# The second network's selection: the mask is written by ScalarE into h's PSUM bank, and the predicated copy moves into the same step

## The chip, the cores and the metric

The kernel runs on one core of a Trainium2 chip. The metric is the device time of one execution in microseconds, from start to end; the median of the runs shown stands for the kernel. The profile is one execution of its own, whose span runs from the first to the last instruction of the program.

## The reference

Three stages follow each other. Attention pools pairs of queries and gives 2304 rows of 512. A router hands each row to one of 8 experts, 288 rows to each, and each expert applies its two matrices. The third stage, the second network, is applied to every row:

```python
def _moe2_ref(x, w_in, w_out):
    h = x @ w_in               # 2304 x 512 by 512 x 2048
    g = h - np.tanh(h)
    return g @ w_out           # 2048 x 512
```

All data are float32. The kernel keeps that precision by splitting each factor of a product into a high and a low part and adding three products.

## The kernel before

After attention the kernel takes the experts one by one. For each of the 8 it runs the expert's own two products (class FFN, `h1` and `y`) and then the second network on the expert's 288 rows. This second part is called a round here: round 0 is that of the first expert, round 7 that of the last. A round has 16 steps; step f handles 128 of the 2048 columns of h, as a tile of 128 partitions by 288 rows.

`stream` (L1067) sets TensorE's order. In step f it issues `stage_a` (12 products that leave h of step f in a PSUM bank; called A(f) here), then `stage_b` for the elementwise work, and from step 3 on `ostep(f - 3)` (12 products with the output weights, added up in four other banks; O(f - 3) here). TensorE's order is therefore A(0) A(1) A(2) A(3) O(0) A(4) O(1) and so on; O(13) to O(15) follow in the next expert's first products, and in the last round at the very end (`finale`). The banks of h come from a pool with two buffers (`hps`, L902): A(f + 2) can start only when everything that reads or writes the bank of step f is through.

The elementwise work finds g = h - tanh(h). The plain difference is exact enough only where h is large; elsewhere a polynomial in z = h² is used, and a predicated copy puts the difference over the polynomial where z is above T0². For one step the instructions are:

- ScalarE: z (L956), hc, a copy of h into SBUF (L957), th = tanh(h) (L958), s, the square of z plus a constant (L959), all read in that order; then gh, the high part of g (L975, the tile `ah`).
- GpSimd: th = hc - th (L960), and the low part of g (L976, the tile `al`; on VectorE in the very last step).
- VectorE: p in three products, called P1 (L961, reads hc and z), P2 (L965, reads z and p) and P3 (L967, reads s and p); the mask mk (L966); and the predicated copy SEL (L973).

`stage_b` calls `stage_c(f - 1)` after P1 of step f. So VectorE's order within a step is P1(f), SEL(f - 1), P2(f), mk(f), P3(f), ScalarE's is z(f), hc(f), th(f), s(f), gh(f - 1), and GpSimd's is th(f), low part of g(f - 1). Each engine takes its queue strictly in the order of the program.

Between the steps of a round the same engines carry other work: the router's search for the next expert's rows (VectorE, with some small products on TensorE and `sat` on ScalarE, in rounds 0 to 5), the next expert's gather (`gather`, L848, issued by GpSimd), its transposes (`xpose`, L859) and splits of weights (`split_w`, L838). Rounds 0 to 5 are called loaded here, rounds 6 and 7 quiet.

Of the kernel before, what the change touches and what calls it, by code (L numbers as in the profile page):

```python
# [10 lines left out]
F32 = mybir.dt.float32  # L11
F32R = mybir.dt.float32r
BF = mybir.dt.bfloat16
I32 = mybir.dt.int32
AF = mybir.ActivationFunctionType
OP = mybir.AluOpType
# [16 lines left out]
T0 = 0.45  # L33
LEAD = -0.018649105653569312
# [16 lines left out]
class Attention:  # L51
# [51 lines left out]
        self.t[P] = dict(kr=kr, qr=qr)  # L103

    def warm(self, n):
        """Products that nobody reads: the tensor engine's clock is slow until it has been busy for a while."""
        ps = self.t["warm"]
        for _ in range(n):
            self.nc.tensor.matmul(ps[:, 0, :128], self.idle, self.idle, start=True, stop=True)
# [295 lines left out]
class Router:  # L405
# [89 lines left out]
                                  skip_group_check=True)  # L495

    def warm(self, n):
        """Products that nobody reads: the tensor engine's clock slows down when it idles."""
        ps = self.spare()
        for _ in range(n):  # L500
            self.nc.tensor.matmul(ps[:, :128], self.ones, self.after, start=True, stop=True)
# [11 lines left out]
        v.tensor_tensor(A, key, km[:, :, None].to_broadcast([128, n, E]), op=OP.is_equal)  # L513

    def half(self, cs):
        """The start of the first search, for some of the tokens."""
        v = self.nc.vector
        n, K = len(range(TC)[cs]), 2 ** self.LEVELS0[0][1] - 1
        v.tensor_copy(self.Lm[:, cs], self.lg[:, cs])
        self.best(cs)  # L520
        v.tensor_tensor(self.G0[:, cs], self.m[:, cs, None].to_broadcast([128, n, K]),
                        self.top0.bitcast(F32)[:, None, :].to_broadcast([128, n, K]), op=OP.is_ge)
# [269 lines left out]
class FFN:  # L792
# [88 lines left out]
        self.x = xh, xl  # L881

    def mm3(self, steps, mode):
        """steps: (out, (w hi, w lo), (x hi, x lo), first of its sum, last of its sum); mode: what of it comes late."""
        n = len(steps)
        order = {"": [(j, p) for j in range(n) for p in range(3)],
                 "wx": [(j, p) for p in range(3) for j in range(n)],
                 "x": [(j, p) for j in range(n) for p in (0, 2)] + [(j, 1) for j in range(n)],
                 "w": [(j, p) for j in range(n) for p in (0, 1)] + [(j, 2) for j in range(n)]}[mode]
        seen = [0] * n  # L890
        for m, (j, p) in enumerate(order):
            if 2 * m == 3 * n:
                yield
            out, (wh, wl), (xh, xl), first, last = steps[j]
            self.nc.tensor.matmul(out, wl if p == 2 else wh, xl if p == 1 else xh, start=first and not seen[j],  # L895
                                  stop=last and seen[j] == 2)
            seen[j] += 1
# [54 lines left out]
    def stage_b(self, f, ps):  # L952
        nc = self.nc
        z, th, h, p = self.tmp("z", 2), self.tmp("th", 2), self.tmp("hc"), self.tmp("p", 2)
        s = self.tmp("s")
        nc.scalar.activation(z, ps, AF.Square)  # L956
        nc.scalar.activation(h, ps, AF.Copy)  # L957
        nc.scalar.activation(th, ps, AF.Tanh)  # L958
        nc.scalar.activation(s, z, AF.Square, bias=self.bias)  # L959
        nc.gpsimd.tensor_sub(th, h, th)  # L960
        nc.vector.scalar_tensor_tensor(p, h, LEAD, z, op0=OP.mult, op1=OP.mult)  # L961
        if f:
            self.stage_c(f - 1)
        mk = self.tmp("mk")
        nc.vector.scalar_tensor_tensor(p, z, ROOT, p, op0=OP.add, op1=OP.mult)  # L965
        nc.vector.tensor_scalar(mk.bitcast(I32), z, T0 * T0, None, op0=OP.is_gt)  # L966
        nc.vector.scalar_tensor_tensor(p, s, QUAD[1], p, op0=OP.add, op1=OP.mult)  # L967
        self.t[f] = p, mk, th

    def stage_c(self, f, quick=False):  # L970
        nc = self.nc
        p, mk, th = self.t.pop(f)
        nc.vector.copy_predicated(p, mk.bitcast(I32), th)  # L973
        gh, gw = self.g[f] = self.pair()
        nc.scalar.activation(gh, p, AF.Copy)  # L975
        (nc.vector if quick else nc.gpsimd).tensor_sub(gw, p, as32(gh))  # L976
# [30 lines left out]
            yield "e", 2  # L1007

    def finale(self, f):
        """The last step of the last expert's sums, and its rows' way out."""  # L1010
        nc = self.nc
        oT = self.wk.tile([128, DC, CAP], F32, name="oT", tag="yl")
        ps = [self.psum.tile([128, 512], F32, name=n, bufs=b) for n, b in (("ax2", 1), ("h", 2), ("h", 2))]
        g = self.g.pop(f)
        copies = (nc.scalar.copy, nc.vector.tensor_copy)
        cut = lambda d: slice(d * 128, d * 128 + 128)
        row = lambda j: slice(j * 96, j * 96 + 96)

        def turn(ds):
            for j in range(3):  # L1020
                for d in ds:
                    nc.tensor.transpose(ps[j][:96, cut(d)], oT[:, d, row(j)], self.ident)

        step = lambda d: (self.acc[d], (self.wo[0][:, f, cut(d)], self.wo[1][:, f, cut(d)]), g, False, True)
        for ds in ((0, 1), (2,), (3,)):
            for _ in self.mm3([step(d) for d in ds], "x"):
                pass
            for d in ds:
                if d < DC - 1:
                    copies[d % 2](oT[:, d], self.acc[d])  # L1030
                else:
                    for j in range(3):
                        nc.scalar.copy(oT[:, d, row(j)], self.acc[d][:, row(j)])
            if ds[0]:
                turn((ds[0] - 2,))
        turn((2, 3))
        for j in range(3):
            orow = self.wk.tile([96, DM], F32, name="orow", tag="row", bufs=3)
            copies[j % 2](orow, ps[j][:96])
            nc.gpsimd.memset(self.spacer, 0.0)  # L1040
            st = nc.gpsimd.indirect_dma_start(
                out=self.out, out_offset=bass.IndirectOffsetOnAxis(ap=self.pids[:, j:j + 1], axis=0),
                in_=orow, in_offset=None)
            for s in self.stores:
                self.tc.declare_no_dep(st.ins, s, reason="other rows")
            self.stores.append(st.ins)
# [159 lines left out]
def build(ctx, tc, q, k, v, w_gate, w1, w2, w_in, w_out, out):  # L1206
    nc = tc.nc
# [5 lines left out]
    ident = cst.tile([128, 128], F32, name="ident")  # L1213
    make_identity(nc, ident)
    lg = cst.tile([128, TC, E], F32, name="lg")
    bias = cst.tile([128, 1], F32, name="bias")
    spacer = cst.tile([1, 1], F32, name="spacer")
    with ExitStack() as c2:
        psum = c2.enter_context(tc.tile_pool(name="psA", bufs=1, space=bass.MemoryType.PSUM))
# [4 lines left out]
        def weights():  # L1224
            nc.gpsimd.memset(iw, 0.0)
            for s in range(2):
                r = slice(64 * s, 64 * s + 64)
                nc.gpsimd.tensor_copy(iw[r, :, s, :D], ident[r, None, r].to_broadcast([64, HP, D]))
                nc.sync.dma_start(iw[r, :, s, D:], w_gate.rearrange("(hp s d) e -> s d hp e", s=2, d=D)[s])
            nc.vector.memset(bias, QUAD[0])  # L1230
            router.fill()

        at.begin, at.later = weights, router.setup
# [48 lines left out]
```

## Time and profile before

| | us |
|---|---|
| median of 3 runs (1432.44 to 1438.55) | 1432.45 |
| span of the profiled execution | 1429.9 |
| TensorE products busy in it | 1266.8 (89%) |
| VectorE busy | 1189.8 (83%) |
| GpSimd busy | 787.2 (55%) |
| ScalarE busy | 663.1 (46%) |

The profiled execution's own time is its span; the median lies 2.55 us above it, which is what stands around the first and the last instruction. Busy products are not products at their peak rate: the records' ends are modelled, and the granted clock of TensorE (mean 0.946 over the span) sets their pace. The page's 40 slices show TensorE at 80% or more of most slices, and VectorE at 80 to 90% until the last 200 us, where it falls to 50 to 70%.

### The profile page before, as it was taken

What the parts mean: (1) busy time and instruction counts of PE and PEld (TensorE: products, weight loads), DVE (VectorE), ACT (ScalarE), POOL (GpSimd) and SP (SyncE); (2) the same over time, 40 slices, a digit from 0 to 9 for tenths busy, and PEclk for the clock granted to TensorE, in tenths of its full rate; (3) what the DMA queues carried; (4) which work ended last, traced back from release to release, by engine and by line L of the source; (5) the groups of instructions that cost most, each with busy time, mean ns of one, the idle gap of its engine ahead of it and who ended that gap; (6) DMA issues with size and microseconds to landing.
All of it is one profiled execution on the core that took longest, in us unless ns stands there. A gap on an engine that the chain in (4) does not pass through costs nothing.

```text
span 1429.9 us, 26773 instructions
## 1 busy us (share of the span) xinstructions
PE 1266.8 (89%) x9379; PEld 1097.6 (77%) x9379; DVE 1189.8 (83%) x2500; ACT 663.1 (46%) x1700; POOL 787.2 (55%) x688
## 2 busy tenths in 40 slices
PE   7888889898888988957989999989899899899997
PEld 6666666566666666647889989889799899898996
DVE  6898988888888889986797897997977978958665
ACT  3444445354444544512445444454454444545554
POOL 4666666756666766612355364553643553646544
PEclk8989999899999999978999999999999999999999
DMA  8887888887778877335832013102111220131200
GB/s 207 198 202 184 188 200 200 192 181 173 192 188 197 191 187 183 100 107 170 302 113 81 18 55 99 44 26 84 54 46 54 55 80 19 54 112 48 83 9 18
DMA packets 164967, 175.02 MB, mean 122 GB/s; under 512 B 66400, under 2 KB 117600, under 8 KB 164832
## 3 DMA queue, kind: packets, MB, share of 16 engines
q1 hardware_dynamic: 161760, 163.86, 45.1%
q0 software_dynamic: 3072, 9.44, 2.2%
q8 instruction: 74, 1.21, 0.4%
q14 instruction: 61, 0.50, 0.1%
HBM read 100.16 MB, written 26.21 MB: 88 GB/s over the span
## 4 chain that ended last, share of the span: by engine, by line
PE 42%; DVE 37%; issue 10%; ACT 6%; POOL 3%; DMA 2%; SPq 1%; DVEq 0%; POOLq 0%; ACTq 0%
PE acc L895 10%; PE h L895 8%; PE pv L235 6%; DVE p L961 5%; DVE pm L196 5%; PE aux L192 4%; DVE p L973 4%; PE sc L218 3%; PE sc L217 3%; ACT ah L975 3%; DVE p L967 2%; DVE db L778 2%; DVE q L186 2%; DVE G L483 2%; POOL al L976 1%
## 5 line engine op out<-in xcount | busy, mean ns | idle before, releaser
L227 POOL TENSOR_TENSOR acc<-acc,E 128x576 f32<-128x576 f32 x217 | 319.5, 1497 | 70.5 <-ACT E L219 69.3
L219 ACT ACTIVATE E<-sc 128x288 f32<-128x288 f32 x576 | 219.2, 413 | 253.3 <-PE sc L218 227.6
L196 DVE TENSOR_REDUCE pm<-aux 128x1 f32<-128x384 f32 x432 | 216.8, 546 | 34.3 <-PE aux L192 31.9
L895 PE MATMUL h<-yh,wi 128*128 128x288 f32 x1024 | 228.8, 304 | 0.0
L976 POOL TENSOR_TENSOR al<-p,ah 128x288 fp32r<-128x288 f32 x127 | 128.5, 1012 | 162.0 <-ACT ah L975 162.0
L218 PE MATMUL sc<-q,k 128*128 128x288 f32 x576 | 178.1, 316 | 43.7 <-DVE q L186 43.6
L217 PE MATMUL sc<-q,k 128*128 128x288 f32 x576 | 189.7, 336 | 1.8 <-ACT E L219 1.8
L960 POOL TENSOR_TENSOR th<-hc,th 128x288 f32<-128x288 f32 x128 | 120.5, 942 | 121.0 <-ACT th L958 118.6
L895 PE MATMUL acc<-ah,wo 128*128 128x288 f32 x1024 | 170.0, 307 | 10.2 <-ACT ah L975 10.1
L895 PEld LDWEIGHTS h<-yh,wi 128*128 128x128 f32 x1024 | 174.1, 193 | 0.5
L192 PE MATMUL aux<-kh,qz 128*128 128x384 f32 x432 | 155.8, 377 | 20.2 <-DVE pm L196 12.0
L235 PE MATMUL pv<-E,vr 128*64 128x288 f32 x1152 | 173.7, 424 | 0.0
L895 PEld LDWEIGHTS acc<-ah,wo 128*128 128x128 f32 x1024 | 146.9, 194 | 28.5 <-issue 13.9
L975 ACT ACTIVATE ah<-p 128x288 fp32r<-128x288 f32 x128 | 56.9, 445 | 210.7 <-DVE p L973 210.7
L218 PEld LDWEIGHTS sc<-q,k 128*128 128x128 f32 x576 | 117.5, 204 | 48.0 <-DVE q L186 48.0
L895 PE MATMUL h<-yl,wi 128*128 128x288 f32 x512 | 149.4, 300 | 0.0
L217 PEld LDWEIGHTS sc<-q,k 128*128 128x128 f32 x576 | 116.8, 203 | 22.9 <-issue 15.5
L192 PEld LDWEIGHTS aux<-kh,qz 128*128 128x128 f32 x432 | 80.6, 192 | 64.7 <-DVE pm L196 38.2
L961 DVE SCALAR_TENSOR_TENSOR p<-hc,z 128x288 f32<-128x288 f32 x128 | 93.7, 732 | 40.0 <-ACT hc L957 20.6
L845 POOL TENSOR_TENSOR w1l<-w1r,w1h 128x512 fp32r<-128x512 f32 x64 | 83.5, 1307 | 71.2 <-ACT w1h L844 67.5
L235 PEld LDWEIGHTS pv<-E,vr 128*64 128x64 f32 x1152 | 76.2, 139 | 53.2 <-issue 23.4
L895 PEld LDWEIGHTS h<-yl,wi 128*128 128x128 f32 x512 | 97.8, 194 | 0.0
(245 smaller groups left out, 2721.6 us busy)
## 6 DMA issues: line engine op xcount, KB each, us to landing
k<-kh SPq DMA_DIRECT2D x64, 288.0 KB, 5.1
w1r<-in_moe_w_dram SPq DMA_DIRECT2D x64, 256.0 KB, 2.9
w2r<-in_moe_w_dram SPq DMA_DIRECT2D x64, 256.0 KB, 2.8
q<-qh SPq DMA_DIRECT2D x64, 144.0 KB, 2.6
k<-kl SPq DMA_DIRECT2D x32, 288.0 KB, 5.5
vr<-in_v_dram SPq DMA_DIRECT2D x16, 576.0 KB, 6.5
qr<-in_q_dram SPq DMA_DIRECT2D x30, 288.0 KB, 8.2
kr<-in_k_dram SPq DMA_DIRECT2D x30, 288.0 KB, 9.1
```

The costliest lines, as they stand in the source:

```text
L192: nc.tensor.matmul(ps, qz[:, blk * 128:blk * 128 + 128], kh[:, pc * 384:pc * 384 + 384], start=True, stop=True)
L196: nc.vector.tensor_reduce(pm[:, blk, pc:pc + 1], ps, axis=AX.X, op=OP.max)
L217: nc.tensor.matmul(ps, t["k1"][s][:, ks], t["q1"][:, s, qs], start=True, stop=False)
L218: nc.tensor.matmul(ps, t["k2"][s][:, ks], t["q2"][:, s, qs], start=False, stop=True)
L219: nc.scalar.activation(e[:, hf], ps, AF.Exp, scale=1.0 / 16.0)
L227: eng.tensor_add(a, a, e)
L235: nc.tensor.matmul(t["pv"][64 * s:64 * s + 64, hf, :HALF], t["vr"][:, s, c, :], t["E", c, s][:, hf], start=(c == 0), stop=(c == KC - 1), s ...
L895: self.nc.tensor.matmul(out, wl if p == 2 else wh, xl if p == 1 else xh, start=first and not seen[j], stop=last and seen[j] == 2)
L960: nc.gpsimd.tensor_sub(th, h, th)
L961: nc.vector.scalar_tensor_tensor(p, h, LEAD, z, op0=OP.mult, op1=OP.mult)
L975: nc.scalar.activation(gh, p, AF.Copy)
L976: (nc.vector if quick else nc.gpsimd).tensor_sub(gw, p, as32(gh))
```

## The change

In `stage_b` the predicated copy of step f is issued in step f, as the last of VectorE's work on it, and `stage_c(f - 1)` (now only gh and the low part of g) moves ahead of s(f) on ScalarE and ahead of th(f) on GpSimd. P1 reads h from its PSUM bank in place of hc. The mask mk on VectorE is removed: ScalarE writes relu(z - T0²) over h in h's own bank, and the predicated copy reads its bits from there. The copy hc stays, since GpSimd's subtraction reads it. The biases of s and of the new mask are given as numbers; the tile `bias` gets a second column and one more memset at the start of the kernel. Comments are emptied.

```diff
@@ stage_b @@
         nc.scalar.activation(z, ps, AF.Square)
         nc.scalar.activation(h, ps, AF.Copy)
         nc.scalar.activation(th, ps, AF.Tanh)
-        nc.scalar.activation(s, z, AF.Square, bias=self.bias)
-        nc.gpsimd.tensor_sub(th, h, th)
-        nc.vector.scalar_tensor_tensor(p, h, LEAD, z, op0=OP.mult, op1=OP.mult)
         if f:
             self.stage_c(f - 1)
-        mk = self.tmp("mk")
+        nc.scalar.activation(s, z, AF.Square, bias=QUAD[0])
+        nc.gpsimd.tensor_sub(th, h, th)
+        nc.vector.scalar_tensor_tensor(p, ps, LEAD, z, op0=OP.mult, op1=OP.mult)
+        nc.scalar.activation(ps, z, AF.Relu, bias=-T0 * T0)
         nc.vector.scalar_tensor_tensor(p, z, ROOT, p, op0=OP.add, op1=OP.mult)
-        nc.vector.tensor_scalar(mk.bitcast(I32), z, T0 * T0, None, op0=OP.is_gt)
         nc.vector.scalar_tensor_tensor(p, s, QUAD[1], p, op0=OP.add, op1=OP.mult)
-        self.t[f] = p, mk, th
+        nc.vector.copy_predicated(p, ps.bitcast(I32), th)
+        self.t[f] = p
@@ stage_c @@
-        p, mk, th = self.t.pop(f)
-        nc.vector.copy_predicated(p, mk.bitcast(I32), th)
+        p = self.t.pop(f)
         gh, gw = self.g[f] = self.pair()
@@ build @@
-    bias = cst.tile([128, 1], F32, name="bias")
+    bias = cst.tile([128, 2], F32, name="bias")
...
-            nc.vector.memset(bias, QUAD[0])
+            nc.vector.memset(bias[:, 0:1], QUAD[0])
+            nc.vector.memset(bias[:, 1:2], -T0 * T0)
```

## Rows read from the trace of the kernel before

**Rows 1.** Windows: stretch, length; busy (count) of PE, PEld, DVE, ACT, POOL; PEclk, DMA.
```profile
1093.39:1152.46 59.07, 52.24 (x402) 50.40 (x400) 55.18 (x134) 29.64 (x83) 32.38 (x33) 0.94 0.12 34
1284.38:1332.14 47.76, 44.67 (x338) 44.13 (x337) 39.59 (x77) 29.04 (x81) 30.33 (x32) 1.00 0.14 43
1368.06:1412.63 44.57, 44.57 (x336) 44.25 (x334) 34.63 (x73) 26.40 (x74) 25.50 (x28) 1.00 0.01 2
```

**Rows 2.** Waits of PE, 1093 to 1152: total us, times, longest.
```profile
PE aux L545 <- ACT sat L540: 2.9, 1, 2.9
```

**Rows 3.** Waits of PE, 1284 to 1332.
```profile
PE ax L866 <- DVE xl L878: 3.1, 1, 3.1
```

**Rows 4.** Groups by line from 575 us on: busy us, mean ns, idle before.
```profile
L961 DVE SCALAR_TENSOR_TENSOR p<-hc,z 128x288 f32<-128x288 f32 x128 | 93.7, 732 | 40.0 <-ACT hc L957 20.6 <-POOL al L976 19.3
...
L966 DVE TENSOR_SCALAR mk<-z 128x288 int32<-128x288 f32 x128 | 39.3, 307 | 0.0
...
L917 DVE SCALAR_TENSOR_TENSOR al<-h,ah 128x288 fp32r<-128x288 f32 x64 | 29.1, 455 | 49.5 <-ACT ah L916 49.3
```

**Rows 5.** Timeline, start of round 7: start us, us, engine, instruction, idle before.
```profile
1368.66 0.42 ACT L958 ACTIVATE th<-h 128x288 f32<-128x288 f32 x1
...
1368.81 0.46 DVE L961 SCALAR_TENSOR_TENSOR p<-hc,z 128x288 f32<-128x288 f32 x1 [1.44 <-ACT hc L957]
...
1369.16 0.80 POOL L960 TENSOR_TENSOR th<-hc,th 128x288 f32<-128x288 f32 x1 [11.55 <-ACT th L958]
...
1369.30 0.98 DVE L965 SCALAR_TENSOR_TENSOR p<-z,p 128x288 f32<-128x288 f32 x1
...
1370.42 0.45 DVE L967 SCALAR_TENSOR_TENSOR p<-s,p 128x288 f32<-128x288 f32 x1
...
1372.78 1.32 PE L895 MATMUL acc<-ah,wo 128*128 128x288 f32 x8
```

**Rows 6.** Timeline, a step of round 7.
```profile
1373.81 0.80 POOL L960 TENSOR_TENSOR th<-hc,th 128x288 f32<-128x288 f32 x1
1373.88 1.05 DVE L961 SCALAR_TENSOR_TENSOR p<-hc,z 128x288 f32<-128x288 f32 x1 [0.70 <-POOL al L976]
...
1374.85 0.48 DVE L973 COPY_PREDICATED p<-mk,th 128x288 f32<-128x288 int32 x1
...
1375.36 0.45 ACT L975 ACTIVATE ah<-p 128x288 fp32r<-128x288 f32 x1 [1.31 <-DVE p L973]
...
1375.81 0.45 DVE L967 SCALAR_TENSOR_TENSOR p<-s,p 128x288 f32<-128x288 f32 x1
...
1375.88 1.04 POOL L976 TENSOR_TENSOR al<-p,ah 128x288 fp32r<-128x288 f32 x1 [1.28 <-ACT ah L975]
```

**Rows 7.** Timeline of DVE, round 4: P3 of steps 1 and 2.
```profile
1098.34 0.45 DVE L967 SCALAR_TENSOR_TENSOR p<-s,p 128x288 f32<-128x288 f32 x1
...
1101.48 0.45 DVE L967 SCALAR_TENSOR_TENSOR p<-s,p 128x288 f32<-128x288 f32 x1
```

**Rows 8.** Timeline of DVE, round 4: step 7, and P1 of step 8.
```profile
1117.66 0.44 DVE L961 SCALAR_TENSOR_TENSOR p<-hc,z 128x288 f32<-128x288 f32 x1
1118.03 0.47 DVE L973 COPY_PREDICATED p<-mk,th 128x288 f32<-128x288 int32 x1
...
1118.98 0.44 DVE L967 SCALAR_TENSOR_TENSOR p<-s,p 128x288 f32<-128x288 f32 x1
...
1126.07 0.45 DVE L961 SCALAR_TENSOR_TENSOR p<-hc,z 128x288 f32<-128x288 f32 x1
```

**Rows 9.** Timeline of PE, round 4: tally products, and O(8).
```profile
1128.44 0.43 PE L494 MATMUL aux<-G,A 128*8 128x63 bf16 x9
...
1135.45 2.08 PE L895 MATMUL acc<-ah,wo 128*128 128x288 f32 x8
```

**Rows 10.** Windows (columns as in group 1), just after that wait.
```profile
1135.72:1139.12 3.40, 3.40 (x17) 3.39 (x17) 3.30 (x12) 1.43 (x5) 1.35 (x2) 0.50 0.01 5
```

**Rows 11.** Timeline of PE, the last O.
```profile
1417.80 0.79 PE L895 MATMUL acc<-ah,wo 128*128 128x288 f32 x4
```

## The prediction

> **What bounds the kernel now.** The change touches only the eight rounds of the second network, so I read the windows of the rounds first (from a round's first z to its last). In round 7 TensorE is never idle: 336 products in 44.57 us, 0.133 each, so 12 of them take 1.59 and a step (A and O) 3.18 [rows 1]. Round 6 is nearly the same. A loaded round, of which there are six, takes 59.07: VectorE is busy for 55.18 of them and TensorE for 52.24, at a mean clock of 0.94 [rows 1]. So two limits have to be kept apart: in quiet rounds TensorE, with the elementwise chain just keeping up; in loaded rounds VectorE's queue, for which TensorE waits in a few places, the longest 2.9 us for `sat` [rows 2]. Next I read the groups by line, for what each operation costs and whether something stretches it, and then the timelines of a round's start, of a quiet step and of loaded steps, for the order and the gaps.
>
> **Two facts about VectorE decide the sum.** First, an instruction with two SBUF inputs and a GpSimd subtraction exclude each other. P1 (two SBUF inputs) starts at 1373.88 while th runs until 1374.61, and ends at 1374.93, 0.32 after it, after 1.05 us [rows 6]; the mean of P1 is 732 ns where the undisturbed one takes 440 to 450 [rows 4, 8]. It holds the other way round as well: the low part of g starts at 1375.88 during P3 and ends at 1376.92, 0.66 after P3 [rows 6]. An instruction with one input in PSUM is free of this: 64 of L917 have a mean of 455 [rows 4]. Second, an instruction that doesn't need its predecessor's result starts before that one ends (SEL at 1118.03, P1 before it until 1118.10), while one that does starts after the end (P2 of step 0 at 1369.30, its P1 until 1369.27) [rows 5, 8]: 0.07 ahead against 0.03 behind.
>
> **What is removed and moved on VectorE.** mk goes: 307 ns [rows 4], but by starts only about 0.22 of VectorE's time. In exchange the order becomes P1, P2, P3, SEL, each needing the one before, where SEL of the previous step and mk stood between them until now. Block before, P1's start to P3's end: 1117.66 to 1119.42, 1.76 [rows 8]. Block after: 0.46 + 0.45 + 0.45 + 0.48 and three gaps of 0.03 to 0.04, 1.94 [rows 5, 6, 8]. So the block gets 0.18 longer, although it has one instruction fewer. What is won is that P1 no longer stands still behind GpSimd.
>
> **What is added on ScalarE.** The mask is one pass over 288 elements from SBUF. No row shows a write to PSUM by ScalarE; the nearest is gh, 0.45 [rows 6], and I take that; below it, 0.3, above it, 0.55. At either end ScalarE, busy for 29.6 of 59 us [rows 1], has room. But the mask waits for P1, and behind it in ScalarE's queue stand z of the next step, `sat` and the weights' splits. Before, gh(f - 1) held the same queue until SEL(f - 1), which came after P1(f); so this wait ends no later. s without its bias tile costs the same or less. The extra memset is one instruction outside the rounds, below 0.2 us. No DMA and nothing on SP moves.
>
> **The wait that is new.** SEL(f) now needs th(f) from GpSimd in the same step, and th(f) stands there behind the low part of g(f - 1), and behind any gather or split. Behind SEL wait all router instructions on VectorE. And A(f + 2) needs h's bank, which now is free after SEL(f) instead of after tanh(f). I follow this at three places.
>
> *Start of a round* (round 7, time from its first z at 1368.06 [rows 1]): tanh ends at 1.02, th runs on GpSimd from 1.10 to 1.90, P1 today starts at 0.75 [rows 5]. After: P1 takes h's bank after ScalarE's last read, 1.06 to 1.52; P2 is held by th and ends at 1.90 + 0.32 = 2.22; P3 to 2.71; SEL 2.75 to 3.23. A(2) starts at 3.27. (If the program lets P1 read h beside tanh, P1 starts at 0.44, behind z, SEL(0) ends at about 2.9, and the lateness found below is 2.9 in place of 3.2; I take 3.2, the order of one engine after the other on one bank.) Step 1: gh(0) to 3.71; P1 3.2 to 3.65; P2 to 4.15; low part of g held by P2, to 4.81; P3 to 5.13; th to 5.79; SEL to 6.33. A(3) runs from 6.37 to 7.96, then O(0). Today O(0) starts at 4.72 [rows 5], with A(1) to A(3) without a gap. TensorE is 3.2 us late, in two gaps of about 1.6.
> The Trainium skill, "PSUM — Partial Sum Buffer", section "PSUM bank collisions raise a hardware error", says that ScalarE and VectorE must not read one bank at the same time, which speaks against P1 on h beside tanh. No row shows such a pair; by this rule the later of the two starts above is the right one, and the sum stays.
>
> *A quiet step:* from the end of SEL(f - 1): gh to 0.48, P1 beside it to 0.39, P2 0.42 to 0.87, low part of g to 1.53, P3 to 1.85, th to 2.51, SEL to 3.05 to 3.2 by the order in which P3 and th get through. TensorE needs 3.18. So the chain just keeps up, and TensorE's lateness from the start stays to the end.
>
> *A loaded round.* Where the router has about 1 us of work in a step, today's step is 3.14 [rows 7]. After, P2 and P3 come to lie where the low part of g and th run: SEL ends 3.35 to 3.43 after the last SEL; I take 3.4, 0.26 more. Where the router has 2 us or more, GpSimd is done in time and the step is longer by the block alone, 0.18. Up to step 8 of round 4 there are four of each: 1.04 + 0.7. At step 0 VectorE is through at 3.23 instead of 2.81 (end of P3(0), 1370.87 [rows 5]), 0.4 more. Today P3(8) ends one block of 1.76 after 1126.07, that is 34.4 us into the round [rows 1, 8]; after, SEL(8) at 36.6. A(10) has to wait for it; then come O(7) and A(11), three times 1.59, and 1.3 of tallies and transposes (two tallies of 0.43 [rows 9] and as much again for the rest, an estimate): O(8) at 42.7. Today O(8) starts at 1135.45, 42.1 into the round [rows 9], because TensorE had stood for `sat` before. That wait goes, and the one for SEL(8) takes its place: 0.6 us late per loaded round.
>
> **The clock.** After the 2.9 us wait the granted clock was 0.50 for 3.4 us (the lower of the two levels, 1.2 GHz) [rows 10], which costs 1.7. After the 3.1 us wait of round 6 none fell: 1.00 throughout [rows 1, 3]. The two new gaps at a round's start add up to 3.2, the size of both; one of two is half, so I take 0.85 for each of 8 rounds (0 to 1.7).
>
> **The sum.** Six loaded rounds: 6 x 0.6 = 3.6. Round 7: TensorE late by 3.2, but its last O waits for gh today and starts at 1417.80 [rows 11]; A(15) ends 24 times 1.59 behind O(0) at 1372.78 [rows 5], at 1411.0; after, 3.2 later, and O(12) to O(14) follow without waiting, three times 1.59: 1419.0, 1.2 late. Round 6: 3.2, of which its 3.1 us wait [rows 3] can take up to all; half, 1.5. Clock: 8 x 0.85 = 6.8. Together 13.1. The profiled execution's span of 1429.9 becomes 1443.0, the median, 2.55 above it, about 1445. Low end: no clock loss, light steps at 3.1, round 6 at nothing: 1431. High end: light steps at 3.5, the lower clock in every round, 3.2 in round 6, and 1 us per loaded round where the next expert's first product waits for SEL(14): 1463.
>
> **Rivals.** *VectorE's relief wins (1417).* Per round mk is 16 x 0.307 = 4.9 and the excess of P1 is 16 x (0.732 - 0.455) = 4.4 [rows 4]. If the gaps between dependent instructions did not matter, a loaded round had 9.3 us less on VectorE; less the 3.2 of the start, half of the rest reaching TensorE, 3 per round: 18 gained, 2.7 lost in rounds 6 and 7. For it: VectorE is the fullest engine there. Against it: the starts in rows 5 and 8. The Trainium skill, "VectorE: DVE Perf Modes", "Rules for kernel authors", states for chained operations that a drain happens regardless and that the number of operations is to be made small; by this rule the shorter list is the faster one, and the rows on starts speak against it. Chance 0.22.
> *The waits only change places (1435).* The lateness of the start is taken up by the waits that TensorE has anyway, and the clock falls as often as now: 1432.45 + 1.2 + 1.5. For it: 6.8 us of idle TensorE in the loaded round. Chance 0.28, with anything from 1425 to 1439.
> *My forecast, slower (1445):* the mechanism is h's bank, held until SEL; it decides as soon as SEL(f) ends over 4.8 us (three times 1.59) after A(f), or A(2) would otherwise have followed at once. Chance 0.50.
> That the change doesn't do what it says, the mask costing ScalarE 0.55 in place of 0.45, alters none of these.
>
> **How the numbers follow.** 0.5% is about what a measurement of this kernel can tell from no change: 7.2 us, 1425.3 to 1439.6. Faster 0.22, same 0.28, slower 0.50. The range leaves out the best part of the first rival and the tip of the last: 1420 to 1460; the likeliest case's own range is 1431 to 1463.
>
> **What would show it.** In the trace after: A(2) and A(3) waiting for SEL (L973's successor) at the start of all eight rounds, O(0) near 8 us; P1 never over 0.5 us; P2 and P3 stretched to about 1 us in light steps; the wait for `sat` gone and one of some 4 us for SEL at step 8; round 7 at 47 to 48 us between first and last z plus its lag. Wrong would be: P2 starting before P1 ends, loaded rounds under 56 us, or A(2) following at once.

## The result, and the profile after

The changed kernel takes **1439.95 us** (median of 12 runs, 1434.93 to 1445.46) against 1432.45 of the kernel before, measured beside it: a ratio of **1.0053, 95% interval 1.0034 to 1.0071**. It is slower, by about as much as a measurement of this kernel can tell from no change. Its profiled execution spans 1438.9 us, 9.0 more than the one before. The attention part moves by up to 10 us from profile to profile (the first z of round 0 lies between 694.5 and 705.2 us in the kernels below), so I count from that z to the end: 729.7 us before, 739.3 after, **9.6 more**. From round to round the differences are +2.6, +1.0, +1.6, +0.1, +0.1, +0.6 for the loaded rounds 0 to 5, -0.1 for round 6 and +3.7 for round 7.

The windows of rounds 4, 6 and 7 from first to last z, with the columns of [rows 1] (length; busy us and count of PE, PEld, DVE, ACT, POOL; granted clock; DMA):

```profile
1098.10:1158.33 60.23, 52.94 (x421) 50.29 (x420) 52.26 (x119) 35.04 (x97) 30.18 (x33) 0.94 0.12 33
1289.81:1337.64 47.83, 44.82 (x338) 44.10 (x337) 39.25 (x63) 33.19 (x96) 30.64 (x33) 1.00 0.14 42
1373.35:1421.92 48.57, 46.17 (x326) 45.59 (x325) 37.32 (x59) 30.62 (x89) 26.22 (x29) 0.93 0.01 1
```

In the loaded round VectorE has 2.9 us less to do than in [rows 1], yet the round is 1.2 longer: VectorE now stands idle for 8.0 of its 60.2 us, against 3.9 of 59.1. The relief is there, and something eats it. The waits of PE in rounds 4 and 6 (total us, times, longest):

```profile
PE h L895 <- DVE p L967: 7.3, 5, 3.5
...
PE h L895 <- DVE p L967: 3.0, 2, 1.9
```

The wait for `sat` [rows 2] and round 6's wait of 3.1 [rows 3] are gone. In both rounds all that is listed is the first product of an A that waits for SEL, now line 967, to free h's bank. The groups by line from 575 us on, for [rows 4] (busy us, mean ns, idle before):

```profile
L962 POOL TENSOR_TENSOR th<-hc,th 128x288 f32<-128x288 f32 x128 | 123.0, 961 | 95.0 <-ACT th L958 95.0
L975 POOL TENSOR_TENSOR al<-p,ah 128x288 fp32r<-128x288 f32 x127 | 111.9, 881 | 204.9 <-ACT ah L974 196.8 <-PE acc L895 7.6
L966 DVE SCALAR_TENSOR_TENSOR p<-s,p 128x288 f32<-128x288 f32 x128 | 103.5, 809 | 13.4
L965 DVE SCALAR_TENSOR_TENSOR p<-z,p 128x288 f32<-128x288 f32 x128 | 94.3, 737 | 4.4
L967 DVE COPY_PREDICATED p<-h,th 128x288 f32<-128x288 int32 x128 | 62.4, 488 | 24.8 <-POOL th L962 9.7
L963 DVE SCALAR_TENSOR_TENSOR p<-h,z 128x288 f32<-128x288 f32 x128 | 57.6, 450 | 24.5 <-ACT th L958 24.0
...
L961 ACT ACTIVATE s<-z 128x288 f32<-128x288 f32 x128 | 56.2, 439 | 0.0
L964 ACT ACTIVATE h<-z 128x288 f32<-128x288 f32 x128 | 52.9, 414 | 69.1 <-DVE p L963 68.2
```

SEL, P2 and P3 of before, which [rows 4] does not show:

```profile
L973 DVE COPY_PREDICATED p<-mk,th 128x288 f32<-128x288 int32 x128 | 82.3, 643 | 0.8
...
L965 DVE SCALAR_TENSOR_TENSOR p<-z,p 128x288 f32<-128x288 f32 x128 | 63.4, 495 | 0.3
...
L967 DVE SCALAR_TENSOR_TENSOR p<-s,p 128x288 f32<-128x288 f32 x128 | 58.9, 460 | 0.0
```

P1 (L963) has a mean of 450 ns in place of 732 and a longest of 0.46 us: GpSimd never holds it any more. SEL, whose mask now lies in PSUM, falls from 643 to 488. P2 and P3 (L965, L966) are held instead, 737 and 809 ns in place of 495 and 460, since th and the low part of g now run beside them. So of the 95.3 us that mk, P1 and SEL are spared in the eight rounds, P2 and P3 take 75.5 back. The mask costs 414 ns on ScalarE, and s without its bias tile 439.

The idle time in round 4 has its own rows (P3, P2, SEL, P1):

```profile
L966 DVE SCALAR_TENSOR_TENSOR p<-s,p 128x288 f32<-128x288 f32 x15 | 12.2, 816 | 1.6
L965 DVE SCALAR_TENSOR_TENSOR p<-z,p 128x288 f32<-128x288 f32 x15 | 10.2, 679 | 0.5
L967 DVE COPY_PREDICATED p<-h,th 128x288 f32<-128x288 int32 x14 | 6.8, 486 | 1.8
L963 DVE SCALAR_TENSOR_TENSOR p<-h,z 128x288 f32<-128x288 f32 x15 | 6.7, 448 | 2.4 <-ACT th L958 2.4
```

Ahead of P2, P3 and SEL, each behind the one whose result it needs, VectorE stands idle for 3.9 us in all, where it had none before; that is nearly the whole of the 4.1 us by which its idle time in the round grew.

The start of round 7 (start us, us, engine, instruction, idle before):

```profile
1373.95 0.42 ACT L958 ACTIVATE th<-h 128x288 f32<-128x288 f32 x1
...
1374.40 0.46 DVE L963 SCALAR_TENSOR_TENSOR p<-h,z 128x288 f32<-128x288 f32 x1 [1.74 <-ACT th L958]
1374.45 0.80 POOL L962 TENSOR_TENSOR th<-hc,th 128x288 f32<-128x288 f32 x1 [11.55 <-ACT th L958]
...
1374.90 0.66 DVE L965 SCALAR_TENSOR_TENSOR p<-z,p 128x288 f32<-128x288 f32 x1
...
1375.66 0.46 DVE L966 SCALAR_TENSOR_TENSOR p<-s,p 128x288 f32<-128x288 f32 x1
...
1376.25 0.48 DVE L967 COPY_PREDICATED p<-h,th 128x288 f32<-128x288 int32 x1
...
1376.79 0.40 PE L895 MATMUL h<-yh,wi 128*128 128x288 f32 x1 [1.88 <-DVE p L967]
...
1379.78 0.61 PE L895 MATMUL h<-yh,wi 128*128 128x288 f32 x1 [0.52 <-DVE p L967]
```

P1 takes the bank 0.03 after tanh, P2 follows it by 0.04, P3 stands 0.10 behind P2 and SEL 0.13 behind P3; the next A has to wait for SEL twice. The windows of two of the seven stretches at the lower clock, from the first z on:

```profile
1132.00:1138.80 6.80, 5.48 (x35) 5.21 (x36) 5.13 (x10) 4.69 (x14) 4.01 (x5) 0.50 0.05 14
1377.80:1384.60 6.80, 6.28 (x27) 5.93 (x26) 4.50 (x7) 3.56 (x12) 3.31 (x5) 0.50 0.00 1
```

There are seven of 6.8 us. In rounds 0 to 4 one begins some 34 us in, during the wait of 3.5 us for SEL of step 8; in round 5 one begins at 30.4 us, during a wait of 4.1 for the router (`tot`); the last stands at the start of round 7. Before there were ten of 3.4 us like [rows 10]. Half of the 47.6 us against half of the 34.0 is 6.8 us more, and that is the most that the clock can have cost: TensorE was busy in 39.5 us of these stretches and waited in the rest, where before it was busy in nearly all of them. By the busy time alone the clock cost 2.8 us more.

### The profile page after: what moved, and what is told of

Its sections match the earlier page's. It is cut to its first block, busy times and chain, and to the rows that moved or that the text cites. A ratio compares the mean times of both kernels' runs of the same rounds, so it can differ in the third digit from the quotient of the medians.

```text
span 1438.9 us, 26644 instructions
## 1 busy us (share of the span) xinstructions
PE 1267.3 (88%) x9379; PEld 1096.2 (76%) x9379; DVE 1170.4 (81%) x2373; ACT 704.5 (49%) x1828; POOL 765.1 (53%) x688
## 4 chain that ended last, share of the span: by engine, by line
PE 42%; DVE 21%; issue 21%; POOL 9%; DMA 3%; ACT 3%; SPq 2%; POOLq 0%; DVEq 0%; ACTq 0%
PE h L895 10%; PE acc L895 9%; PE pv L235 6%; PE aux L192 5%; DVE pm L196 4%; POOL th L962 4%; PE sc L217 4%; PE sc L218 4%; POOL al L975 3%; DVE db L778 2%; DMA qr<-in_q_dram 1%; PE aux L164 1%; PE aux L298 1%; DVE q L186 1%; DVE G L483 1%
## 5 line engine op out<-in xcount | busy, mean ns | idle before, releaser
L895 PE MATMUL h<-yh,wi 128*128 128x288 f32 x1024 | 238.3, 312 | 47.1 <-DVE p L967 47.1
L975 POOL TENSOR_TENSOR al<-p,ah 128x288 fp32r<-128x288 f32 x127 | 111.9, 881 | 204.9 <-ACT ah L974 196.8
L895 PEld LDWEIGHTS h<-yh,wi 128*128 128x128 f32 x1024 | 177.2, 196 | 55.8 <-DVE p L967 54.7
L966 DVE SCALAR_TENSOR_TENSOR p<-s,p 128x288 f32<-128x288 f32 x128 | 103.5, 809 | 13.4
L186 DVE TENSOR_TENSOR q<-ident,nm 64x320 fp32r<-64x320 f32 (+1 forms) x64 | 98.0, 1532 | 1.6
```

The source lines that it names most:

```text
L186: nc.vector.tensor_mul(dv[oth[s], bs, hf, :], self.ident[r, None, r].to_broadcast([64, n, 64]), nm[r, bs, None].to_broadcast([64, n, 64]))
```

## The experiments

The theories were, in short: *the bank* (h's bank is held until SEL, TensorE starts every round late: my prediction), *dependent starts* (P1, P2, P3, SEL one behind the other cost VectorE what mk's removal saves), and against them *VectorE's relief* (P1 without GpSimd's hold is what counts). To compare them I read one quantity throughout: round 4 from its first to its last z, split into VectorE's busy and idle time.

| kernel | ratio to before | interval | round 4, us | VectorE busy | idle |
|---|---|---|---|---|---|
| before | 1 | | 59.07 | 55.18 | 3.89 |
| P1 from PSUM alone | 0.9877 | 0.9854–0.9900 | 54.54 | 51.25 | 3.29 |
| ScalarE's mask alone, in SBUF | 1.0015 | 0.9994–1.0036 | 59.46 | 52.61 | 6.85 |
| both | 0.9921 | 0.9895–0.9947 | 56.45 | 50.13 | 6.32 |
| both, SEL(f-1) ahead of P1(f) | 0.9921 | 0.9891–0.9952 | 56.61 | 52.85 | 3.76 |
| both, SEL(f) in its own step, th first | 1.0039 | 1.0018–1.0059 | 58.63 | 52.93 | 5.70 |
| both, SEL(f) in its own step | 1.0030 | 1.0013–1.0047 | 57.64 | 51.62 | 6.02 |
| the change (mask in h's bank) | 1.0053 | 1.0034–1.0071 | 60.23 | 52.26 | 7.97 |

**The bank freed after P1.** In the changed kernel the mask goes into a tile in SBUF.

```diff
-        nc.scalar.activation(ps, z, AF.Relu, bias=-T0 * T0)
+        mk = self.tmp("mk")
+        nc.scalar.activation(mk, z, AF.Relu, bias=-T0 * T0)
-        nc.vector.copy_predicated(p, ps.bitcast(I32), th)
+        nc.vector.copy_predicated(p, mk.bitcast(I32), th)
```

> The changed kernel with one edit: ScalarE writes the mask into an SBUF tile, so h's bank is free after P1(f) and not after SEL(f); order and number of instructions stay. My theory (the bank held until SEL is the cause): A(2) of a round starts at about 1.6 us in place of 3.4, O(0) at 5.5 to 6.5 in place of 8.4, the wait of A(10) at step 8 ends at P1's end, 1.7 us earlier; the half-clock stretch at the start of round 7 is gone; 1433 to 1436 us against the 1440 of the change. Rival (the longer chain SEL, gh, low part of g, th, SEL through GpSimd is the cause, whoever holds the bank): as the change, 1438 to 1442, since SEL now has two SBUF inputs and shares VectorE's lock with GpSimd.

Measured 1437.9 us, 1.0030. In round 7 A(2) follows at once (1.56 us after the first z, 3.44 in the changed kernel), and O(0) of a loaded round starts at 5.97 us in place of 8.39. Of the 3.4 us by which TensorE starts late (O(0) at 5.01 before), 2.4 are gone in rounds 1 to 5, and only about 0.2% comes back, with intervals that overlap. From round to round this profile is 0.8 to 1.5 us shorter than the changed kernel's in rounds 0 to 4; against that, round 6 is 4.1 longer, with a wait of 3.6 us for `xl` and a stretch of 6.8 at half speed that the changed kernel doesn't have there. So the late start exists as predicted, but with it gone the kernel is still slower than before: it is not the main cause of the loss.

**th ahead of the low part of g on GpSimd**, in the changed kernel:

```diff
+        nc.gpsimd.tensor_sub(th, h, th)
         if f:
             self.stage_c(f - 1)
         nc.scalar.activation(s, z, AF.Square, bias=QUAD[0])
-        nc.gpsimd.tensor_sub(th, h, th)
```

> The changed kernel with one edit: GpSimd subtracts th(f) before the low part of g(f - 1), so SEL(f) no longer waits for gh and the low part of the step before. My theory: A(2) unchanged (3.4), A(3) about 0.9 earlier, SEL(f) 0.5 to 0.9 earlier in every light step, no gain at step 8; 1435 to 1438. Rival (GpSimd's order is the whole cause): round starts near the old ones and 1433 or less. Rival (the order is without weight, the bank alone counts): 1440.

Measured 1438.34 us, 1.0030 (1.0015 to 1.0046). TensorE's waits for SEL sum up to 47.8 us, as in the changed kernel (47.1). So it is not th's place behind the low part of g that makes SEL late.

**P1 from PSUM, alone**, in the kernel before:

```diff
-        nc.vector.scalar_tensor_tensor(p, h, LEAD, z, op0=OP.mult, op1=OP.mult)
+        nc.vector.scalar_tensor_tensor(p, ps, LEAD, z, op0=OP.mult, op1=OP.mult)
```

> The kernel before with one part of the change alone: P1 reads h from PSUM; mask, SEL and order as before. My theory: P1 is never stretched by GpSimd any more (0.45 in place of a mean of 0.73), VectorE has 4 us less per round, but h's bank is held until P1 (about 1.5 to 2.3 us after z in place of 1.0, 6.7 at step 8); together little: 1429 to 1433. Rival (VectorE's relief decides): 4.4 us less on VectorE in each of six loaded rounds, half of it reaching the end: 1419 or less.

Measured **1417.34 us, 0.9877**: one operand, and 1.2% faster than the kernel before. I had given it next to nothing. Its window of round 4:

```profile
1087.28:1141.82 54.54, 50.73 (x402) 48.53 (x400) 51.25 (x134) 29.32 (x82) 31.82 (x33) 0.97 0.13 37
```

Its group of P1 from 575 us on:

```profile
L961 DVE SCALAR_TENSOR_TENSOR p<-h,z 128x288 f32<-128x288 f32 x128 | 57.7, 451 | 52.4 <-ACT th L958 45.2 <-POOL al L976 6.3 <-ACT s L959 0.9
```

VectorE has 3.9 us less to do in the round, its idle time stays, and the round is 4.5 shorter: in a loaded round what VectorE is spared reaches the end, if its idle time doesn't grow. P2 and P3 are not held in exchange (498 and 488 ns in this round). The clock goes from 0.94 to 0.97 with it: four stretches at half speed instead of ten are left. At 1.7 us each these six are some 10 of the 19.4 us by which this profile is shorter from the first z on, so up to half of the gain may come by way of TensorE's clock.

**ScalarE's mask, alone**, in SBUF, in the kernel before (mk on VectorE is dropped, `nc.scalar.activation(mk, z, AF.Relu, bias=...)` takes its place):

```diff
+        nc.scalar.activation(mk, z, AF.Relu, bias=-T0 * T0)
         nc.vector.scalar_tensor_tensor(p, z, ROOT, p, op0=OP.add, op1=OP.mult)
-        nc.vector.tensor_scalar(mk.bitcast(I32), z, T0 * T0, None, op0=OP.is_gt)
```

> The kernel before with another part alone: ScalarE makes the mask (relu of z less the threshold) into the SBUF tile mk, VectorE's mask instruction is gone; SEL stays in the next step. My theory: P3 now follows P2, whose result it needs, directly, and starts 0.1 after its end, where with mk between them it started 0.22 after mk's start; so VectorE's block shrinks by about 0.1 us a step only: 1430 to 1433. Rival (the number of VectorE instructions decides, as in the skill's rule on chained operations): 0.3 us a step, 4.9 a loaded round, half of it at the end: 1418 or less.

Measured 1434.74 us, 1.0015 with 1 inside the interval: no gain, and just above the range that I had given. Its round 4:

```profile
1094.44:1153.90 59.46, 52.92 (x421) 50.91 (x419) 52.61 (x119) 34.35 (x97) 32.21 (x33) 0.94 0.12 33
```

Its group of P3 in this round:

```profile
L967 DVE SCALAR_TENSOR_TENSOR p<-s,p 128x288 f32<-128x288 f32 x15 | 7.3, 487 | 1.6
```

VectorE does 2.6 us less and idles 3.0 more. More than half of the new idle time stands ahead of P3, which now follows directly on P2, whose result it needs (1.6 us in 15 steps, 0.0 in the same round of before): with mk between them, that time had been covered. An instruction fewer is no time less here, as the prediction had read from the starts.

**Both of these** (the two diffs above together; SEL still in the next step):

> The kernel before with two parts of the change: P1 reads h from PSUM, and ScalarE makes the mask (into SBUF); SEL stays in the next step, between P1 and P2. Alone the first gave 0.988 and the second 1.0015 of the time before. Theory M (the move of SEL into its own step is what costs): 1415 to 1420, so the changed kernel with its mask in SBUF (1437.9) differs from this one by the move alone, some 19 us. Theory D (the gaps between adjacent dependent instructions on VectorE cost): P2 and P3 are adjacent here, one gap of three: 1422 to 1426.

Measured 1421.79 us, 0.9921, between the two theories. The mask adds nothing to P1's gain either: the time is 0.4% longer than with P1 from PSUM alone, and the two intervals touch.

**SEL(f-1) ahead of P1(f)**, in the kernel with both:

```diff
-        nc.vector.scalar_tensor_tensor(p, ps, LEAD, z, op0=OP.mult, op1=OP.mult)
         if f:
             self.stage_c(f - 1)
+        nc.vector.scalar_tensor_tensor(p, ps, LEAD, z, op0=OP.mult, op1=OP.mult)
```

> The kernel before with P1 from PSUM and ScalarE's mask in SBUF, and SEL of the step before issued ahead of P1: P1, P2, P3 are adjacent and depend on each other, as in the change, and are open to GpSimd's subtractions as there, but SEL never waits for th, and gh has SEL's result early. Theory D (adjacent dependent instructions, and P2 and P3 stretched by GpSimd): most of the loss comes back, 1428 to 1436. Theory W (SEL's wait for th in its own step, and th behind the low part of g): 1415 to 1420.

Measured 1421.88 us, 0.9921, the same. P1, P2 and P3 stand one behind the other, and it costs nothing that can be measured; but what this adds is only P2 behind P1, 0.03 each, since P3 followed on P2 already. Its window of round 4:

```profile
1090.14:1146.75 56.61, 50.70 (x402) 48.65 (x400) 52.85 (x119) 35.05 (x98) 31.68 (x33) 0.97 0.13 35
```

Its groups in that round:

```profile
L967 DVE SCALAR_TENSOR_TENSOR p<-s,p 128x288 f32<-128x288 f32 x15 | 12.3, 821 | 1.6
L973 DVE COPY_PREDICATED p<-mk,th 128x288 f32<-128x288 int32 x14 | 9.3, 665 | 0.1
L966 DVE SCALAR_TENSOR_TENSOR p<-z,p 128x288 f32<-128x288 f32 x15 | 9.2, 615 | 0.5
L963 DVE SCALAR_TENSOR_TENSOR p<-h,z 128x288 f32<-128x288 f32 x15 | 6.7, 444 | 0.8 <-ACT th L958 0.8
```

P3 is stretched here as in the changed kernel (821 and 816 ns in this round), at 1.3% less time. So the stretch of P2 and P3 is not what the change loses by.

**The move alone**: the kernel with P1 from PSUM, with SEL in its own step, gh and the low part of g ahead of s and th, the mask still VectorE's mk in SBUF.

```diff
+        if f:
+            self.stage_c(f - 1)
         nc.scalar.activation(s, z, AF.Square, bias=self.bias)
         nc.gpsimd.tensor_sub(th, h, th)
         ...
-        if f:
-            self.stage_c(f - 1)
         nc.vector.tensor_scalar(mk.bitcast(I32), z, T0 * T0, None, op0=OP.is_gt)
         nc.vector.scalar_tensor_tensor(p, s, QUAD[1], p, op0=OP.add, op1=OP.mult)
+        nc.vector.copy_predicated(p, mk.bitcast(I32), th)
```

> The kernel before with P1 from PSUM and the move alone: SEL(f) last in its own step, gh and the low part of g of step f - 1 ahead of s(f) and th(f) as in the change; the mask stays on VectorE in SBUF, between P2 and P3, so h's bank is free after P1 and only two adjacent pairs depend on each other. Theory M (the move costs): 1434 to 1442. Theory D (adjacent dependent instructions): about 1428. Bank theory of the prediction (h's bank held until SEL): near 1417, since the bank is not held.

Measured 1468.06 us, 1.0259 (1.0224 to 1.0295): 3.9% behind the kernel that it is taken from, and far outside all three theories. Its group of mk:

```profile
L966 DVE TENSOR_SCALAR mk<-z 128x288 int32<-128x288 f32 x128 | 100.0, 781 | 0.0
```

mk falls under GpSimd's hold in this order, 781 ns against 307 [rows 4], and lies in the chain from SEL to SEL, where a step of round 7 takes 3.24 us. This explains a part: round 4 is 59.38 us here, 4.8 more than without the move. The stretch from a round's last z to the next round's first is longer too, 43.0 us in place of 39.6 behind round 4: TensorE waits there 2.6 us for the router in place of 0.9, and a half-speed stretch of 3.4 us lies in it (granted clock 0.96 against 1.00). What it shows for the change is that mk's way to ScalarE, worth nothing by itself, is needed once SEL moves.

**The bank held longer**: the kernel with both, the mask written into h's bank, SEL left in the next step.

```diff
-        mk = self.tmp("mk")
-        nc.scalar.activation(mk, z, AF.Relu, bias=-T0 * T0)
+        nc.scalar.activation(ps, z, AF.Relu, bias=-T0 * T0)
```

> The kernel before with P1 from PSUM and the mask written by ScalarE into h's PSUM bank, but SEL(f) where it was, in step f + 1 behind P1(f + 1): the bank of h is held a whole step longer than in the change. Bank theory of the prediction: A(f + 2) waits for SEL(f) in nearly every step, round starts 3 us or more late, 1445 or more. If the bank is of little weight (the changed kernel gained only 2 us when its bank came free after P1): 1418 to 1425.

Measured 1505.05 us, 1.0498 (1.0456 to 1.0540). Waits of PE from 575 us to the end:

```profile
PE h L895 <- DVE p L972: 90.8, 89, 4.3
```

So the bank does cost, 5.8% against the kernel with both, when it is held past P1 of the next step. The change holds it for one step less, and there it costs the 0.2% of the first experiment. So in this kernel, with two banks for h, a mask in h's bank is dear unless SEL moves as well.

**hc in two buffers.** In the first experiment's kernel ScalarE waits for GpSimd's th ahead of hc, 77.6 us in all, since hc has one buffer (its group of hc):

```profile
L957 ACT ACTIVATE hc<-h 128x288 f32<-128x288 f32 x128 | 52.4, 410 | 77.7 <-POOL th L962 77.6
```

To make room for a second one the mask is written over z, behind P2:

```diff
-        z, th, h, p = self.tmp("z", 2), self.tmp("th", 2), self.tmp("hc"), self.tmp("p", 2)
+        z, th, h, p = self.tmp("z", 2), self.tmp("th", 2), self.tmp("hc", 2), self.tmp("p", 2)
         ...
-        mk = self.tmp("mk")
-        nc.scalar.activation(mk, z, AF.Relu, bias=-T0 * T0)
         nc.vector.scalar_tensor_tensor(p, z, ROOT, p, op0=OP.add, op1=OP.mult)
+        nc.scalar.activation(z, z, AF.Relu, bias=-T0 * T0)
```

> This is the kernel with ScalarE's mask in SBUF and the predicated copy in its own step (1.0030 of the kernel before), with hc in two buffers; to make room the mask is written over z after P2 instead of into a tile of its own. Theory S (ScalarE's copy hc(f+1) waits for th(f), because hc has one buffer: 77.6 us of idle time in 128 steps there, against 2.7 in the kernel that has only P1 changed, and z(f+1), tanh(f+1) and everything behind them start late): the wait falls below 15 us and most of the 1.1% comes back, 1419 to 1426 us, 0.992 to 0.996. Theory L (the loop SEL, gh, low part of g, th, SEL is what sets the step, and hc's wait only shows it): the wait moves to another place, and the time stays at 1435 to 1440, 1.001 to 1.005.

Measured 1442.29 us, 1.0064 (1.0042 to 1.0087). Its groups of the mask and of hc:

```profile
L965 ACT ACTIVATE z<-z 128x288 f32<-128x288 f32 x128 | 57.0, 445 | 160.0 <-DVE p L964 158.0
...
L957 ACT ACTIVATE hc<-h 128x288 f32<-128x288 f32 x128 | 51.6, 403 | 0.0
```

hc's wait is gone and the time is not: a wait of 158 us now stands ahead of the mask, which in this kernel is written over z and so has to wait for P2. Since the edit itself brought that wait, this kernel alone doesn't decide against theory S. The next one does.

**th first, with the bank free** (the first experiment's kernel with the second's edit), and **the same with hc in two buffers**:

> The kernel with ScalarE's mask in SBUF and the predicated copy in its own step (1.0030), with GpSimd's th(f) put ahead of gh(f-1) and the low part of g(f-1). Against the kernel with the predicated copy at the head of the next step (0.9921) only that copy's place differs now. Theory L in the form that GpSimd's order is the cost (th(f) stands behind the low part of g(f-1), and SEL(f) behind th(f)): 0.992 to 0.996, 1419 to 1427 us. Theory V (SEL in its own step stands in VectorE's queue ahead of the router's work and waits there for th, whatever the order on GpSimd): 1.000 to 1.004, 1432 to 1439 us.

> Both edits of the two kernels beside it: hc in two buffers, the mask over z, and th(f) ahead of the low part of g(f-1) on GpSimd. If either of theories S and L is right, 0.990 to 0.996, 1417 to 1427 us. If the cost is that SEL waits in its own step on VectorE (theory V), 1.000 to 1.004.

Measured 1437.75 us, 1.0039 (1.0018 to 1.0059), and 1436.04 us, 1.0020 (0.9996 to 1.0044). Both lie where theory V had them, though not for its reason, a wait for th. In the first one hc waits for th for only 9.4 us in all, in place of 77.6, and the time stays: theory S falls. This kernel and the one with th first and the mask in h's bank (1.0030) also differ by the bank alone, and here freeing it brings nothing. The first one is the nearest pair to the kernel with SEL ahead of P1: the same operations, the same order on GpSimd, and SEL(f) at the end of its step instead of at the head of the next (beside it, only gh and s change places on ScalarE, and s has its bias as a constant; VectorE shows nothing of that, since the idle time ahead of P3, which reads s, is 1.5 against 1.6 us). The difference is **1.2%**. Its window of round 4:

```profile
1094.89:1153.52 58.63, 50.35 (x398) 48.11 (x397) 52.93 (x117) 33.28 (x97) 29.19 (x34) 0.97 0.12 34
```

Its groups in that round:

```profile
L967 DVE SCALAR_TENSOR_TENSOR p<-s,p 128x288 f32<-128x288 f32 x14 | 10.8, 774 | 1.5
L968 DVE COPY_PREDICATED p<-mk,th 128x288 f32<-128x288 int32 x14 | 9.6, 683 | 1.9
L966 DVE SCALAR_TENSOR_TENSOR p<-z,p 128x288 f32<-128x288 f32 x14 | 8.4, 600 | 0.5
L963 DVE SCALAR_TENSOR_TENSOR p<-h,z 128x288 f32<-128x288 f32 x15 | 6.7, 448 | 1.1 <-ACT th L958 1.1
```

The round is 2.0 us longer. VectorE's work is the same, 52.9; its idle time is 1.9 longer, and 1.8 of this stand ahead of SEL (1.9 against 0.1). No releaser is named, th is long done: SEL starts 0.13 after the end of P3, whose result it needs, 14 times. At the head of the next step the router's instructions lie between the two. From the first z of round 7, without router work, the two kernels take the same 60.8 us. So in the loaded part it is a cost in VectorE's queue, not a wait for GpSimd. From round to round the difference is 2.5 to 3.0 in rounds 0 to 6, and VectorE's queue doesn't explain all of it. Round 6 has no router work and is 2.5 longer too: there the granted clock is 0.97 against 1.00 from first to last z, so that the same 338 products are busy for 46.21 us in place of 44.75, and TensorE waits 2.2 us for `xl` in place of 1.3. The 0.9 beyond the loaded part of round 4 is not followed further. That the price is the start behind P3 is read from round 4's rows; that SEL's place costs 1.2% is measured.

**SEL between P2 and P3**, to take P3's 0.10 away as well, in the kernel with both:

```diff
-        if f:
-            self.stage_c(f - 1)
         mk = self.tmp("mk")
         nc.scalar.activation(mk, z, AF.Relu, bias=-T0 * T0)
         nc.vector.scalar_tensor_tensor(p, z, ROOT, p, op0=OP.add, op1=OP.mult)
+        if f:
+            self.stage_c(f - 1)
```

> The kernel with both of P1 from PSUM and ScalarE's mask in SBUF (0.9921, the predicated copy in the next step), with SEL(f-1) and its gh and low part moved from between P1 and P2 to between P2 and P3, so that P3 no longer stands right behind the instruction whose result it needs. In the kernel it is taken from, VectorE stood idle for 13.7 us ahead of the 128 P3s (0.107 each), and the loaded part of a round was 56.4 to 56.8 us, 50.1 to 50.5 of VectorE's work and 6.3 of idle time. Theory G (the start of a dependent instruction is paid for in the loaded rounds): P3's idle time falls under 3 us in all, P2 gets 0.03 each, the loaded part falls by 1.2 to 1.6 us in six rounds, 1410 to 1415 us, 0.985 to 0.988. Theory T (the idle time is only traded: GpSimd's subtractions stretch VectorE's instructions by what is won, as in the kernel with SEL ahead of P1, which had 2.5 less idle time and 2.5 more work): P3's idle time falls, VectorE's busy time rises by about as much, 1418 to 1425 us, 0.990 to 0.995.

Measured 1455.93 us, 1.0152 (1.0114 to 1.0190): neither theory. The wait of ACT that goes with it, from 575 us to the end (total us, times, longest):

```profile
ACT mk L963 <- DVE p L973: 204.7, 120, 4.8
```

Its group of P3:

```profile
L967 DVE SCALAR_TENSOR_TENSOR p<-s,p 128x288 f32<-128x288 f32 x128 | 56.9, 444 | 0.8
```

P3's idle time did fall, from 13.7 to 0.8 us. But the mask now stands in ScalarE's queue ahead of gh(f-1), and it has one buffer, which SEL(f-1) still reads; so it waits 205 us in all, and gh and the next z stand behind it. I had moved gh past the mask and not counted it. A step of round 7 takes 3.38 us. What P3's gap is worth remains open: SEL's move without that queue, with the mask behind gh, wasn't tried.

## Why the prediction was right, and where its steps were not

**Sign and size.** 1445 was forecast, 1439.95 came; for the profiled execution 13.1 us more were forecast, and 9.6 came from the first z on. By the prediction's own terms, with the clock taken out either as half of TensorE's busy time at the lower level or as half of all the time there (so a range, in which more for the clock is less for the rounds):

| term | forecast | in the trace |
|---|---|---|
| six loaded rounds | +3.6 | +2.6 to +6.4 |
| round 6 | +1.5 | -0.1 |
| round 7 | +1.2 | +0.3 to +0.6 |
| clock | +6.8 | +2.8 to +6.8 |
| sum | +13.1 | +9.6 |

**The start of a round** came as forecast: P1 takes h's bank after tanh (1.05), SEL ends at 3.38 (3.23), A(2) starts at 3.44 (3.27), O(0) at 8.1 to 8.8 us ("near 8"), and at 9.5 in round 7, where the clock fell. But that it matters failed as the main mechanism: with the bank free after P1 the change is still 0.3% behind. Round 6 took its 3.2 up entirely (its wait of 3.1 [rows 3] went, as the low end had it), and the loaded rounds a part of it: with the bank free, rounds 0 to 4 were 0.8 to 1.5 us shorter, not 2.4.

**The order of the four.** The step that an operation less gives VectorE nothing was right (the mask alone: 1.0015), and the rule of the Trainium skill against which it stood ("VectorE: DVE Perf Modes", "Rules for kernel authors", make the number of operations small) isn't borne out here: 2.6 us less work and 3.0 more idle time in the round. The gaps were under-sized: 0.03, 0.10 and 0.13 instead of three of 0.03 to 0.04. The block without any hold is 2.12 us at step 8 of round 4, not 1.94. That P2 and P3 get held was foreseen; that SEL is held less, 643 to 488 ns, was not counted.

**P1's relief** is the term that was missing. The prediction had the number (16 times 0.277, 4.4 us in a round), put it into a rival, let half reach TensorE and set the gaps against it. Alone it shortens round 4 by 4.5 us and the kernel by 1.2%. That rival was right about P1 and wrong about mk. The mechanism is the one of [rows 4 to 6]: with one input in PSUM VectorE is free of GpSimd (451 ns, as L917 had shown). The Trainium skill says the same, "SBUF — State Buffer", section "Who interferes with whom": "A DVE instruction with at most one SBUF input, outside the 2-port perf modes, does not contend with GpSimd".

**SEL's place** is the loss that balances it: about 1.2% in the nearest pair. The prediction counted SEL's move only for the bank and the start; in a loaded round VectorE's own queue pays, 14 to 16 times 0.13, as far as the rows go (round 6 pays too, by a lower clock and a longer wait). So 1.0053 is -1.2% (P1), about +0.4 (the mask, within its uncertainty), +1.1 to +1.2 (SEL's place) and -0.1 to +0.2 (the bank, which can't be told from nothing). The sign and the size came out by luck: the prediction left out two terms of the same size, and they cancel, while the bank, which it held to be the mechanism, gives next to nothing.

**The wait at step 8** was there: 3.5 us for SEL, forecast as some 4, and `sat` no longer waited for. O(8) of round 4 starts 43.8 us into the round, not at 42.7: the products up to it ran at half clock. **The clock** cost at most what was forecast, and at other places: not at the start of each round, only of round 7 (3.4 us at most), and in the loaded rounds in the wait at step 8 (in round 5 in that for `tot`), where a stretch of 6.8 us replaces two of 3.4 (in four of the six rounds) or one. The forecast of 0.85 a round was half of two cases; that its total lies at the end of the measured range is chance.

**The rival that the waits change places** (1435, within 0.5%) is as close as the forecast, 5 us off on the other side: the measured ratio's interval reaches into it. What speaks for it is the absorbed start; what it lacks is the move's price.

## What to carry to other kernels

Where VectorE shares its time with GpSimd, look at each VectorE instruction with two SBUF inputs whose mean exceeds its undisturbed time, and ask whether one input still lies in PSUM: here this was one operand and 1.2%, and the kernel with that edit alone (1417.3 us) beats both versions. Measure the parts of a bundled change apart; here one part gave 1.2% and another took it back. And look at what stands between two instructions that depend on each other: the gap was 0.03 to 0.13 us each here, nothing could be seen of 0.03, and the one try to close the 0.10 brought a larger wait.

## What the runs showed of the hardware

- The start of a dependent VectorE instruction behind its predecessor is not one number: 0.03 to 0.04 us (P2 on P1), 0.10 (P3 on P2), 0.13 (SEL on P3). The 0.10 stands ahead of P3 in every kernel of the series in which it follows on P2: 13.3 to 14.1 us for the 128 of them.
- Waits of TensorE that look alike are not worth the same: to be 2.4 us later at the start of most rounds cost 0.2% or less, the same kind of wait in most of the steps (91 us in 89 waits) 5.8%.
- VectorE's `tensor_scalar` from SBUF to SBUF, with a single input tensor, can also be held by GpSimd: mk's mean went from 307 ns (359 with P1 from PSUM alone) to 781 by its place in the order. The Trainium skill names `tensor_scalar` among the operations that can contend ("SBUF — State Buffer", "Who interferes with whom"); the rows of before did not show it.
- A pass of ScalarE over 288 elements from SBUF took 414 ns into PSUM (the changed kernel) and 435 into SBUF (the first experiment): no price for the bank as such.
